# Moving w_phi's load to ScalarE's queue, reordering the first matmuls and moving filler waits in a one-core attention and FFN mix

## The chip, the cores and the metric

One core of one Trainium2 chip. The metric is the device time of one execution in microseconds (us). Single executions of the same kernel stray by 1 us and more here (59 of the kernel before, in one set, took 289.09 to 291.74), so means of many are compared. A run is in the slow state when it took over 1.5% more than the fastest of the same kernel; only one in this study did (293.71 us, granted clock 0.992), and it is left out of the ratios. A "long" execution below is one of the ordinary, fast state that took about 1 us more than most. Where a ratio of two kernels is given, it is the mean time of the one's fast runs over that of the other's of the same rounds; it is not quite the ratio of the medians quoted beside it.

## The reference

Two branches over the same x (2048 tokens of 640 values) are mixed by a gate for each token:

```python
g = sigmoid((x * gate_w).sum(-1, keepdims=True))
# A: qkv = x @ wqkv, 32 heads of 20; q and k go through w_phi (20x20 for each head);
#    phi = concat(softmax(p), softmax(-p)); kv = sum over s of phi_k v; z = sum over s of phi_k
#    o = (phi_q @ kv) / (phi_q . z + 1e-6); a = o @ wo
# B: b = (silu(x @ w_gate) * (x @ w_up)) @ w_down            (F = 1728)
return g * a + (1 - g) * b
```

## The kernel before

The kernel is one long list of items in a fixed order; a recording layer adds a semaphore wait wherever an item needs another engine's result. What the change touches lies almost all in the first 12 us. x tiles 0 to 3 are loaded as they are and transposed on TensorE (item X), VectorE copies them out of PSUM, and V of these four tiles is built up row by row as the rows of wv land (items U tile.row). Dummy matmuls (H, two each) fill TensorE's time while the loads come.

```python
LOADS = "x0 w0 x1 w1 x2 w2 x3 w3 w4 f0 h k0 k1 t4 k2 k3 k4 t5 ..."     # w: wv rows, h: w_phi, k: transposed wk
ORDER = """
H0 H1 a H2 H3 H4 H5 H6 H7 H8 H12 G X0 H9 H10 U0.0 X1 H11 U1.0 U0.1 U1.1 X2 U2.0 U0.2 U1.2 U2.1
X3 U2.2 U0.3 U1.3 U2.3 U0.4 U1.4 U2.4 V3 Y F0.1 M1 i3 M0 F0.0 M2 V4 M3 M4 K0 ...
"""
# G: gate row transposed; Y: w_phi spread into masked blocks wbd; F: an FFN item; M: wk premultiplied with wbd
XQ = ["sp", "act", "act", "act"]; WQ = ["sp", "sp", "sp", "sp", "act"]     # queues of x tiles and wv rows

def load_phi():
    dma("sp", wph[:, :, :], ...)

def act_waits():                       # item a
    for _ in range(NWAIT):             # 88
        act.wait_ge(tr.sem["pe"], 1)   # met as soon as TensorE has done one thing

def v_out(t, pr):                      # evicts V of tile t, frees its PSUM pair
    copy("act", o, i)
    copy("act", svec[:, t:t + 1], bank(2 * pr + 1, 320, 321))

def kv_end():
    for _ in range(NPEW):              # 24
        pe.wait_ge(tr.sem["pe"], 1)
    ...
```

There are four PSUM pairs. V of tiles 0 to 3 holds all of them, so the first FFN item (F0.1) starts only when V of tile 0 has been evicted. The recording layer never asks for an activation table; the toolchain puts one table load ahead of ScalarE's first activation.

The softmax here doesn't subtract the row's maximum and nothing guards it: scores larger than these inputs give would overflow.

## Time and profile before

| | us |
|---|---|
| median of the first 3 runs | 290.37 (290.0 to 291.07) |
| the profiled execution | 289.45, span 288.2 |
| TensorE busy | 284.9 |
| first FFN matmul starts | 12.10 |
| from there to the start of the last matmul | 274.02 |

The lines that carry the reading stand in the prediction below. A line of the chain of waits is: start, length, what ran or was waited for; a line of the timeline is: start, length, engine, source line, operation, output<-inputs, shape, count, and in brackets the engine's idle time before it with what ended it.

### The profile page before, as it was taken

How to read it: one execution, taken by the hardware profiler on the slowest of the kernel's cores; microseconds unless marked ns; L12 is line 12 of the kernel's file. 1: busy time of each engine (PE TensorE's matmuls, PEld its weight loads, DVE VectorE, ACT ScalarE, POOL GpSimd, SP SyncE). 2: the span in 40 equal slices, each digit the busy share in tenths (PEclk: the TensorE clock that was granted, in tenths of full speed). 3: DMA queues.
4: the chain of work that ended last, by engine and by line, in shares of the span. 5: the costliest groups of instructions: out<-in, count | busy, mean ns of one | idle time of the engine just before them, and what ended most of it. 6: DMA issues, size and time to landing. Idle time of an engine off the chain costs nothing.

```text
span 288.2 us, 4961 instructions
## 1 busy us (share of the span) xinstructions
PE 284.9 (99%) x1975; PEld 174.8 (61%) x1975; DVE 163.5 (57%) x243; ACT 151.6 (53%) x252; POOL 159.8 (55%) x125
## 2 busy tenths in 40 slices
PE   8999999999999999999999999999999999999997
PEld 6567777575644445557775556675554446656776
DVE  2146748577469978679991475970317899100000
ACT  0678768666685566583445753225676552234112
POOL 8286899879545789836633438350753558501000
PEclk9999999999999999999999999999999999999999
DMA  6975789000020498302292002061020006210101
GB/s 209 185 113 125 113 212 369 9 0 3 0 50 0 104 306 152 63 2 50 55 165 63 12 1 50 2 144 47 2 50 0 3 1 123 52 45 0 49 23 48
DMA packets 48944, 21.62 MB, mean 75 GB/s; under 512 B 39384, under 2 KB 48792, under 8 KB 48920
## 3 DMA queue, kind: packets, MB, share of 16 engines
q1 hardware_dynamic: 48190, 20.62, 31.5%
q10 hardware_dynamic: 730, 0.68, 0.7%
q8 instruction: 16, 0.26, 0.4%
q14 instruction: 8, 0.07, 0.1%
HBM read 9.29 MB, written 2.62 MB: 41 GB/s over the span
## 4 chain that ended last, share of the span: by engine, by line
PE 98%; ACT 1%; DVE 0%; issue 0%; ACTq 0%
PE ps L296 97%; PE ps L478 1%; PE ps L308 1%; ACT L314 0%; ACT v1r L314 0%; DVE xT L320 0%; DVE osb L730 0%; ACTq L139 0%; ACT svec L314 0%
## 5 line engine op out<-in xcount | busy, mean ns | idle before, releaser
L324 POOL TENSOR_TENSOR hT<-hT,us 128x512 bf16<-128x512 bf16 (+1 forms) x56 | 65.0, 1173 | 67.0 <-DVE hT L328 50.1
L328 DVE SCALAR_TENSOR_TENSOR hT<-hT,ps 128x512 bf16<-128x512 bf16 (+1 forms) x56 | 37.4, 683 | 69.0 <-ACT hT L314 55.3
L296 PE MATMUL ps<-xT,wg 128*128 128x512 bf16 x260 | 64.6, 379 | 0.4 <-ACT svec L314 0.4
L296 PE MATMUL ps<-xT,wu 128*128 128x512 bf16 x260 | 64.6, 379 | 0.0
L296 PE MATMUL ps<-wd,hT 128*128 128x320 bf16 (+2 forms) x462 | 63.9, 295 | 0.0
L324 POOL TENSOR_TENSOR ph<-eq,qc 128x1320 bf16<-128x1320 bf16 x16 | 42.3, 2645 | 25.6 <-DVE qc L638 20.8
L296 PEld LDWEIGHTS ps<-wd,hT 128*128 128x128 bf16 x462 | 44.5, 98 | 17.4
L296 PE MATMUL ps<-wqk,xT 128*128 128x320 bf16 x320 | 47.7, 299 | 0.0
L314 ACT ACTIVATE hT<-ps 128x512 bf16<-128x512 f32 (+2 forms) x60 | 35.8, 597 | 16.0 <-PE ps L296 15.8
L296 PEld LDWEIGHTS ps<-xT,wu 128*128 128x128 bf16 x260 | 25.5, 98 | 30.6
L314 ACT ACTIVATE us<-ps 128x512 bf16<-128x512 f32 (+1 forms) x56 | 33.5, 598 | 19.2 <-PE ps L296 18.2
L296 PEld LDWEIGHTS ps<-xT,wg 128*128 128x128 bf16 x260 | 25.0, 98 | 28.4 <-ACT oT L314 0.8
L314 ACT ACTIVATE osb<-ps,omg 128x640 bf16<-128x640 f32 (+2 forms) x17 | 12.9, 757 | 55.8 <-PE ps L296 55.8
L324 POOL TENSOR_TENSOR ekr<-ekr,krec 128x1280 bf16<-128x1280 bf16 x16 | 37.4, 2357 | 5.7 <-DVE krec L338 5.7
L296 PEld LDWEIGHTS ps<-wqk,xT 128*128 128x128 bf16 x320 | 30.5, 98 | 13.1 <-issue 0.4
L314 ACT ACTIVATE eq<-ps 128x640 bf16<-128x640 f32 x32 | 22.3, 703 | 20.8 <-POOL ph L324 10.6
L335 DVE TENSOR_REDUCE ksum<-ekr 128x64 f32<-128x1280 bf16 x16 | 23.5, 1471 | 11.7 <-ACT ekr L314 11.7
L314 ACT ACTIVATE ekr<-ps 128x640 bf16<-128x640 f32 x32 | 22.3, 703 | 8.7 <-PE ps L296 8.2
L335 DVE TENSOR_REDUCE qz<-eq 128x64 f32<-128x1280 bf16 x16 | 23.7, 1479 | 2.6 <-ACT eq L314 2.6
L296 PE MATMUL ps<-wvg,xT 128*128 128x320 bf16 (+1 forms) x160 | 24.6, 301 | 0.1
L296 PE MATMUL ps<-wog,oT 128*128 128x320 bf16 (+2 forms) x165 | 24.7, 295 | 0.0
L335 DVE TENSOR_REDUCE qw<-ez 128x64 f32<-128x1280 bf16 x16 | 23.6, 1477 | 0.0
(73 smaller groups left out, 189.8 us busy)
## 6 DMA issues: line engine op xcount, KB each, us to landing
out_dram<-osb SPq DMA_DIRECT2D x15, 160.0 KB, 1.9
wd<-in_B_w_down_dram SPq DMA_DIRECT2D x1, 2080.0 KB, 9.5
wg<-in_B_w_gate_dram SPq DMA_DIRECT2D x1, 1040.0 KB, 9.5
wu<-in_B_w_up_dram SPq DMA_DIRECT2D x1, 1040.0 KB, 10.7
wg<-in_B_w_gate_dram SPq DMA_DIRECT2D x1, 800.0 KB, 5.6
wu<-in_B_w_up_dram SPq DMA_DIRECT2D x1, 800.0 KB, 7.2
wog<-in_A_wo_dram SPq DMA_DIRECT2D x2, 375.0 KB, 7.2
wvg<-in_A_wqkv_dram SPq DMA_DIRECT2D x4, 160.0 KB, 4.0
```

What stands on the lines that cost most here:

```text
L296: last = pe.matmul(o, lhsT=l, rhs=r, start=st, stop=sp_, skip_group_check=sk)
L308: last = pe.transpose(o, i, ident[0:k, 0:k])
L314: return run("act", lambda: act.activation(o, i, func, scale=scale), rd, [o])
L324: return run(e, lambda: eo.tensor_tensor(o, a, b, op), [a, b], [o])
L328: return run("dve", lambda: dve.scalar_tensor_tensor(out=o, in0=a, scalar=s, in1=b, op0=op0, op1=op1), rd, [o])
L335: return run("dve", lambda: dve.tensor_reduce(o, i, AX.X, ALU.add), [i], [o])
L478: last = pe.matmul(bank(2 * pr, 0, P), lhsT=c, rhs=c, start=True, stop=True)
```

## The change

Its intent is to have less in TensorE's way in the first 12 us: w_phi leaves SyncE's queue, so that SyncE issues the transposed loads behind it earlier; the transposes of x tile 2 and of the gate row move forward; and the 88 filler waits leave ScalarE's start and come back as six waits in each of the 14 FFN items of the third stage.

```diff
-NWAIT = 88
-NPEW = 24
+NWAIT = 6
+NPEW = 32
@@ ORDER
-H0 H1 a H2 H3 H4 H5 H6 H7 H8 H12 G X0 H9 H10 U0.0 X1 H11 U1.0 U0.1 U1.1 X2 U2.0 U0.2 U1.2 U2.1
+H0 H1 H2 H3 H4 H5 H6 G H7 H8 X0 H9 H10 U0.0 X1 H11 U1.0 U0.1 X2 U1.1 U2.0 U0.2 U1.2 U2.1
@@ (load_rows and dma now return their event; load_wv keeps it in wv_evs)
     def load_phi():
-        dma("sp", wph[:, :, :], ...)
+        tr._wait("act", dict([wv_evs[3]]))
+        dma("act", wph[:, :, :], ...)
@@ (act_waits and item a are gone)
@@ fitem
+        if bt == 2:
+            for _ in range(NWAIT):
+                act.wait_ge(tr.sem["pe"], 1)
         actop(h, g, ACTF.Tanh, 0.5)
```

More of the change, by code (lines that the diff above doesn't have):

```diff
@@ L366, in load_rows @@
     def load_rows(e, dst, c, c0):
-        dma(e, dst, A_wqkv[c * P:(c + 1) * P, c0:c0 + D])
+        return dma(e, dst, A_wqkv[c * P:(c + 1) * P, c0:c0 + D])
     def load_x(t):
@@ L377, in load_ffn @@
         dma("sp", wu[:, :, c0:c1], B_w_up[:, c0:c1].rearrange("(c p) j -> p c j", p=P))
+    wv_evs = []
     def load_wv(c):
-        load_rows(WQ[c], wvg[:, c, 0:D], c, 2 * D)
+        wv_evs.append(load_rows(WQ[c], wvg[:, c, 0:D], c, 2 * D))
     dma("act", gwr[0:5, :], bass.AP(gate_w.tensor, gate_w.offset, [[P, 5], [1, P]]))
     def load_phi():
-        dma("sp", wph[:, :, :], A_w_phi.rearrange("h e f -> (h e) f").rearrange("(c p) f -> p c f", p=P))
+        tr._wait("act", dict([wv_evs[3]]))
+        dma("act", wph[:, :, :], A_w_phi.rearrange("h e f -> (h e) f").rearrange("(c p) f -> p c f", p=P))
     def load_wt(which, m):
@@ L424, in fills @@
             memset("pool", zh[:, NCH:P], 0.0)
-    def act_waits():
-        for _ in range(NWAIT):
-            act.wait_ge(tr.sem["pe"], 1)
     for i in range(3):
@@ L752, in _build @@
         "f": lambda i: load_ffn(FCUT[i], FCUT[i + 1]), "L": load_late_weights, "T": tail_weights, "J": gates,
-        "Y": w_blocks, "a": lambda: act_waits(), "I": kv_begin, "N": kv_end, "Z": z_row,
+        "Y": w_blocks, "I": kv_begin, "N": kv_end, "Z": z_row,
         "Q": qtile, "A": qsum, "B": qden, "C": qscale, "c": qmul,
```

## The prediction

> **What bounds the kernel now.** I read the engines' busy shares and the chain that ended last on the page first, to see who owns the time:
>
> ```profile
> PE 284.9 (99%) x1975; PEld 174.8 (61%) x1975; DVE 163.5 (57%) x243; ACT 151.6 (53%) x252; POOL 159.8 (55%) x125
> ...
> PE 98%; ACT 1%; DVE 0%; issue 0%; ACTq 0%
> ```
>
> TensorE is busy for 284.9 of 288.2 us and is 98% of the chain. Busy does not mean dense, so I also added up what the 1975 matmuls need at 2.4 columns per ns (what warm rows show: x5 of 512 columns in about 1.07 us) and subtracted that from the distances between their starts. The columns need 279.9 us and the distances exceed that by 5.3 us. By fortieths of the span (7.2 us each) the excess is 2.75, 0.72, 0.18, 0.22 and then about 0.1 to 0.3 each, mostly steady issue cost. So **all that can be won lies in the first 12 us**, some 3 us, 1.2% of the span. The chain of waits in order of time shows that stretch:
>
> ```profile
> 6.48 0.07 PE ps L308
> 6.55 0.02 issue
> 6.57 0.23 DVE xT L320
> 6.80 0.05 issue
> 6.85 1.27 PE ps L296 x8
> ...
> 9.95 1.28 ACT L314
> 11.24 0.01 issue
> 11.25 0.71 ACT v1r L314
> 11.95 0.07 ACT svec L314
> 12.02 0.07 issue
> 12.10 66.26 PE ps L296 x616
> ```
>
> Two holes are to be seen. At 6.55 to 6.85 TensorE has transposed x tile 2 and waits for VectorE to copy it out. From 9.8 to 12.1 the chain leaves TensorE: ScalarE loads its activation table (1.28 us), only then evicts the first V tile (0.71 us), and only that frees the PSUM pair for the first FFN matmul, at 12.10. TensorE's other V matmuls run out meanwhile (the last starts at 11.40 and lasts 0.135), so it stands still for 0.57 us. From 12.10 there is not one hole of 0.1 us.
>
> The timeline of ScalarE and of TensorE, cut at these places:
>
> ```profile
> 6.32 0.44 PE L308 MATMUL ps<-ident,xs 128*128 128x128 bf16 x5
> 6.85 1.27 PE L296 MATMUL ps<-wvg,xT 128*128 128x320 bf16 x8
> ...
> 9.95 1.28 ACT L314 ACT_TABLE_LOAD   x1 [9.95 <-PE ps L296]
> 11.25 0.71 ACT L314 ACTIVATE v1r<-ps 128x640 bf16<-128x640 f32 x1
> ```
>
> The table load is shown as released by TensorE, though a table needs no data. The built program tells why: the 88 waits that the kernel puts on ScalarE are packed two to an instruction, together with the real wait for V tile 0 (semaphore value 34), and all of them stand ahead of the table load; the activation behind it keeps only a trivial wait for value 1.
>
> **What the Trainium skill says.** "ScalarE: Activation LUTs", section "What ACT_TABLE_LOAD costs": about 1283 ns for a load, plus some 1380 ns of drain. The trace agrees with the load (1283 ns) and not with a drain: the activation starts 11 ns after it. "Runtime: NRT & Kernel Launch", section "Instruction fetch mechanics": instructions come in 16 KiB blocks by DMA, mostly hidden. The trace has 16 such packets of 16 KB (0.26 MB, the count fits TensorE) and 8 of 8 KB for other engines; they are not free for DMA: at 14.27 one holds a DMA engine 0.96 us and the transposed weight block 2 lands 3.4 us after its issue, not 2.2. "TensorE: Matmul & The Clock Gate", section "What's actually happening": the window that grants full clock is free-running, so the warm-up point varies. Here starts of 128 columns go from 107 to 55 ns apart at about 5.2 us; one trace cannot show the variation. "DMA: Bandwidth & Descriptors", section "Queues, rings and completion order": SyncE and ScalarE each own a queue row over the same DMA engines, served in turn. The page shows two queues (20.6 and 0.68 MB).
>
> **The change, part by part.**
>
> (1) The order of the first items. Before: ... U1.0 U0.1 U1.1 X2 U2.0; after: U1.0 U0.1 X2 U1.1 U2.0. Tile 2's transposes move ahead of U1.1's two matmuls (0.27 us), so VectorE's copy runs under these. X2 would start at 6.04 (its rows landed at 5.56), the copy (start 0.25 after, 0.22 long, 0.05 to signal) ends at 6.57, U1.1 at 6.59: U2.0 starts at 6.59, not 6.85. **Gain 0.26.** Next limits: wv row 2 landed 6.47 (needed 6.87), x tile 3 at 7.56 (needed 7.70, with 0.10 of latency), wv row 3 at 8.05 (needed 8.25). They hold, x tile 3 barely.
>
> (2) The gate row amid the dummies. Before: 20 dummies, gate transpose at 3.07, x tile 0 at 3.18; after: 14 dummies, gate, 4 dummies. The gate row landed at 2.16, so it is ready when 14 dummies are done (about 0.84+14x0.107=2.34). But x tile 0 lands at 3.08, so X0 cannot start before about 3.18, and U0.0 waits for wv row 0 (landed 4.22, start 4.36). **Gain 0.**
>
> (3) The 88 waits go from ScalarE's start. By themselves they were hidden (about 3.2 to 6.5 us, ScalarE idle till 9.8). But in the changed program the real wait for V tile 0 sits on the activation, behind the table load. The table load now waits only for the w_phi issue and a long finished memset.
>
> (4) w_phi on ScalarE's queue. It is issued when wv row 3 has landed (8.05), and took SyncE 0.78 us to issue. So ScalarE is through at about 8.95, the table is in at 10.24, V tile 0 (its last matmul starts at 9.48 now) is evicted by 10.95, FFN could start at about 11.09. TensorE finishes its V matmuls at 11.53-0.26=11.27. So the hole of 0.57 closes with some 0.17 to spare. **Gain 0.57 if w_phi's issue is not held up.** SyncE issues its transposes up to 0.8 us earlier.
>
> (5) 14 FFN items of the third stage get 6 waits each: 3 instructions of two, some 0.08 us apart, 0.23 us an item. ScalarE is busy there 53.0 of 128.2 us (160 to 288) and mostly waits for matmuls: **cost 0**. They put the instruction count back for the tail (360 before, 359 after).
>
> (6) 8 more waits on TensorE's sequencer after K/V: they ran at 0.106 us per two, so 0.42 us more. The sequencer was still about 8 matmuls (1.1 us) ahead after the first 24, so it stays ahead: **cost 0**.
>
> Sum: 0.26+0.57=0.83 off the span, of which I keep 0.75 for (4)'s thin margin. 290.37-0.75=289.6.
>
> **The rivals.** *The queue issue is held up*: SyncE's first transpose took 3.82 us to issue (5.01 to 8.83) behind a full queue. If ScalarE's issue is slow in the same way, the table load slips beyond 10 us and only 0.26 remains: 290.1. For the rival: w_phi is 640 pieces of 40 bytes. Against: before, both queues issued side by side at 0.43 to 0.45 each, and ScalarE's queue is empty by 8.3. *A transfer takes the hole's place*: at 0.83 us earlier the premultiplications come to wait for transposed weights. Slack before: block 2 0.71 (17.04 against 16.33), block 4 0.56. Without SyncE's earlier issue they would miss by up to 0.3; SyncE's earlier issue and the fetch that delays them, itself tied to TensorE's progress, should move along. Worth: 0.1 to 0.3 us back. w_phi itself is no danger: premultiplication starts at 13.4 and the masked blocks took 1.5 us after it landed. *Fetches in new places* delay transfers by 1 to 1.5 us in mid-kernel; most TensorE waits there were met over 1 us early, so little comes of it. *Nothing changes at all*: would need the table load to stay behind TensorE, which the program's order rules out.
>
> **Range and chances.** The mechanism gives 289.5 to 290.1. The three runs before span 290.0 to 291.07, so a median moves by some 0.4 whatever the kernel, in part perhaps by the warm-up's phase. Range 288.9 to 290.5. 2% is 5.8 us: all the idle time of TensorE is less than that, so faster by 2% is nearly excluded; slower would need a new stall of 6 us in a stream that has slack everywhere after 12 us.
>
> **What would show it.** Right: the table load starts at about 9.0, released by the w_phi issue and not by TensorE; the first FFN matmul follows the last V matmul without a hole at about 11.3; U2.0 starts near 6.6; the span is near 287.4. (2) is right if X0 still starts at 3.15 to 3.2. Wrong: table load after 9.5; a hole before the premultiplications at 13 to 18.5; TensorE's gaps near 77 us (from the 8 waits) or in the third FFN stage; or a late warm-up that hides the whole difference.

## The result, and the profile after

The changed kernel took 289.27 us by the median of 6 runs (288.67 to 289.71), the kernel before 290.72 (290.0 to 291.73); ratio 0.9944, 95% interval 0.9918 to 0.997. Its output is correct. By the verdict at 2% it is "same". The profiled execution of the changed kernel has a span of 287.5 us.

The page's busy shares and chain of the changed kernel:

```profile
PE 284.5 (99%) x1973; PEld 174.5 (61%) x1973; DVE 163.5 (57%) x243; ACT 151.8 (53%) x252; POOL 159.8 (56%) x125
...
PE 98%; DMA 1%; SPq 0%; DVE 0%; issue 0%
```

ScalarE is gone from the second line: its 1% was the table load and the first eviction. Its chain of waits in order of time, from x tile 2 on:

```profile
6.32 0.28 PE ps L308 x5
6.60 1.37 PE ps L296 x10
7.97 0.28 PE ps L308 x5
8.25 69.40 PE ps L296 x640
```

Neither VectorE's copy (it stood at 6.57) nor ScalarE's load (it stood at 9.95) is in it: TensorE runs from x tile 2 onward without leaving the chain. The timeline of the changed kernel shows the pieces:

```profile
7.64 0.41 ACTq L350 DMA_DIRECT2D wph<-in_A_w_phi_dram  x1
...
8.14 1.28 ACT L314 ACT_TABLE_LOAD   x1 [8.14 <-DMA wvg<-in_A_wqkv_dram]
...
9.66 0.71 ACT L314 ACTIVATE v1r<-ps 128x640 bf16<-128x640 f32 x1 [0.24 <-PE ps L296]
...
11.39 1.24 PE L296 MATMUL ps<-xT,wg 128*128 128x512 bf16 x5
...
11.73 1.49 POOL L324 TENSOR_TENSOR wbd<-wph,bmask 128x160 bf16<-128x160 bf16 x3 [4.58 <-DMA wph<-in_A_w_phi_dram]
...
13.54 0.79 PE L296 MATMUL ps<-wbd,wT 128*128 128x140 bf16 x12
```

The table load is released by the landing of a wv row now (the wait ahead of w_phi's issue), is done before V of tile 0 is, and the first FFN matmul follows the last V matmul (started at 11.25, 0.134 long) at once, at 11.39. Before it was 12.10. One line gives warning: w_phi landed at 11.65, 1.0 us *later* than before, and the masked blocks made of it were done 0.32 us before the premultiplication at 13.54 read them.

The span fell by 0.7 us; the medians of six runs by 1.45 us. That is nearly twice the holes that the prediction counted (0.83), so either part of the gain lay elsewhere or the six runs were lucky.

### The profile page after: what moved, and what is told of

It is laid out like the page before. It is cut to its first block, busy times and chain, and to the rows that moved or that the text cites. A ratio compares the mean times of both kernels' runs of the same rounds, so it can differ in the third digit from the quotient of the medians.

```text
span 287.5 us, 4960 instructions
## 1 busy us (share of the span) xinstructions
PE 284.5 (99%) x1973; PEld 174.5 (61%) x1973; DVE 163.5 (57%) x243; ACT 151.8 (53%) x252; POOL 159.8 (56%) x125
## 4 chain that ended last, share of the span: by engine, by line
PE 98%; DMA 1%; SPq 0%; DVE 0%; issue 0%
PE ps L296 97%; DMA wvg<-in_A_wqkv_dram 1%; PE ps L308 0%; SPq L350 0%; DVE osb L732 0%; PE ps L477 0%
```

## The experiments

My theory: the gain is the two holes (0.57 us behind the table load, 0.26 us at x tile 2) and nothing else, and the rest of 1.45 us is chance. Rivals: w_phi's way gives part of it; the filler waits cost by their own time; the waits move instruction fetches to better places; the gate row's new place counts. All twelve kernels gave the right result. In each call the kernels share a chip and the runs of the kernel before: 59 runs of 289.78 us median in the first, 58 of 289.78 in the second, 51 of 289.89 in the third, 19 of 290.06 in the last.

What the 14 traces have in common made them easy to read. In 11 of them the distance from the first FFN matmul to the start of the last matmul is 274.01 or 274.02 us, in the other three 274.36, 274.39 and 274.88. So executions differ in how late the first FFN matmul starts, in two kinds of wait behind it, and, once, in the end. (A hole below is the distance between the starts of two matmuls, less what the columns of the first need. "Half clock until" is the end of the last distance at half rate: 107 ns for 128 columns, and 55 ns after.)

| kernel | wv row 0 landed | half clock until | hole at x tile 2 | hole before FFN | first FFN matmul | from there to the last |
|---|---|---|---|---|---|---|
| before | 4.22 | 5.17 | 0.26 | 0.57 | 12.10 | 274.02 |
| before again | 4.16 | 5.32 | 0.26 | 0.57 | 12.10 | 274.02 |
| order only | 5.14 | 8.91 | 0 | 0.57 | 14.07 | 274.01 |
| two waits | 3.88 | 4.92 | 0 | 0.55 | 12.67 | 274.02 |
| no waits | 4.18 | 6.35 | 0.26 | 0 | 12.02 | 274.02 |
| order back | 4.14 | 3.98 | 0.26 | 0 | 11.51 | 274.02 |
| changed | 4.35 | 5.29 | 0 | 0 | 11.39 | 274.02 |
| changed again | 4.40 | 3.88 | 0 | 0 | 11.13 | 274.39 |
| gate back | 3.92 | 3.86 | 0 | 0 | 11.08 | 274.36 |
| w_phi on SyncE | 4.14 | 3.91 | 0 | 0 | 11.45 | 274.88 |
| spread waits undone | 4.93 | 8.97 | 0 | 0 | 13.45 | 274.02 |
| w_phi earlier | 3.94 | 5.21 | 0 | 0 | 11.00 | 274.02 |
| w_phi earlier, dummies | 4.75 | 4.28 | 0 | 0 | 11.41 | 274.02 |
| fewer dummies | 3.85 | 6.02 | 0 | 0 | 12.55 | 274.02 |

### Order back

```diff
-U1.0 U0.1 X2 U1.1 U2.0
+U1.0 U0.1 U1.1 X2 U2.0
```

> The changed kernel with tile 2's transposes back behind U1.1. The theory of the two holes: 0.26 us of the gain is lost, so it is 0.57 us faster than the kernel before where the changed one is 0.83 (by the profile) and U2.0 waits 0.26 us for VectorE's copy again. Rival: the measured gain of 1.45 us (medians) is larger than the two holes because something else, w_phi's way, gives the rest; then this one stays about 1.2 us faster than before.

Measured: 289.49 us median (22 runs), ratio 0.9986 (0.9971 to 1.0), so 0.41 us faster than before, with an interval of 0 to 0.84. The hole at x tile 2 is back, in the timeline of TensorE:

```profile
5.92 0.44 PE L308 MATMUL ps<-ident,xs 128*128 128x128 bf16 x5
6.45 0.45 PE L296 MATMUL ps<-wvg,xT 128*128 128x320 bf16 x2
7.09 1.00 PE L296 MATMUL ps<-wvg,xT 128*128 128x320 bf16 x6 [0.20 <-DMA wvg<-in_A_wqkv_dram]
```

The third line shows where such a gain can go. Here wv row 2 landed at 7.05 and TensorE waited for it right behind the hole, so closing the hole would have won nothing in this execution. The mean lies on the theory's side (0.57) of the rival's 1.2, which the interval excludes.

### Two waits

The changed kernel with two always met waits on ScalarE, recorded ahead of its first activation.

```diff
+    def act_waits():
+        for _ in range(2):
+            act.wait_ge(tr.sem["pe"], 1)
-H0 H1 H2
+H0 H1 a H2
```

> The changed kernel with two waits on ScalarE that are always met, ahead of the first eviction. The theory: they are packed with the real wait for V tile 0, all stand ahead of the table load, so the load starts only when TensorE has finished V tile 0 (about 9.5 us), and the hole of 0.57 us before the first FFN matmul is back: 0.26 us faster than the kernel before. Rival (the 88 waits cost by their own time, not by where they put the table load): two waits are 0.08 us, and nothing changes against the changed kernel, 1.45 us faster than before.

Measured: 289.9 us, ratio 1.0008 (0.9993 to 1.0023): the gain is gone. The chain of waits:

```profile
1.73 4.79 DMA wvg<-in_A_wqkv_dram
...
10.52 1.28 ACT L314
11.80 0.01 issue
11.82 0.71 ACT v1r L314
12.52 0.07 ACT svec L314
12.59 0.08 issue
12.67 66.26 PE ps L296 x616
```

The table load is behind TensorE again, with the same 1.28 and 0.71 us after it and the same hole of 0.55 us. Two waits of together less than 0.1 us do what 88 did, so it is not their own time. In the built program of this kernel (the list of each engine's instructions that the toolchain makes, with the semaphore values they wait for) the real wait for V of tile 0 is packed into the instructions ahead of the table load and the activation keeps "at least 1"; in the changed kernel it is on the activation. The rival is excluded. The mean came out 0.23 us slower than before, not 0.26 faster; the interval's faster end is 0.20, so the 0.26 of the order of items is not seen in this mean. This execution lost 0.82 us to wv row 1, which landed at 6.52.

### No waits

```diff
-NWAIT = 88
+NWAIT = 0
```

This is the kernel before, with nothing else changed.

> The kernel before with the 88 waits taken away and nothing else: the table load moves to about 3.3 us. The theory: the hole of 0.57 us closes, 0.57 us faster than before, the wait of 0.26 us at x tile 2 stays. Rival (w_phi's way or the spread waits give the gain): less than 0.3 us.

Measured: 289.55 us (14 runs), ratio 0.999 (0.9969 to 1.0012), which is 0.29 us faster and leaves both readings open. The trace decides. The timeline of ScalarE:

```profile
5.01 1.28 ACT L314 ACT_TABLE_LOAD   x1 [5.01 <-POOL v1r L342]
10.30 0.71 ACT L314 ACTIVATE v1r<-ps 128x640 bf16<-128x640 f32 x1 [4.00 <-PE ps L296]
```

Without the waits the table is in at 6.3 and ScalarE then waits 4 us for V. The hole before the FFN is 0. Taking the waits away is by itself enough; w_phi's way is not needed for it. (The load came at 5.0 rather than 3.3: a memset of GpSimd's stands ahead of it.)

### Order only

The kernel before with X2 ahead of U1.1.

> The kernel before with tile 2's transposes ahead of U1.1 and nothing else. The theory: 0.26 us faster than before, and the hole before the first FFN matmul stays at 0.57 us. Rival (the hole behind the table load is set by something that does not move with TensorE): the hole grows to 0.83 us and nothing is gained.

Measured: 289.84 us (14 runs), ratio 1.0001 (0.9987 to 1.0016): no gain by the mean; the interval, 0.38 us faster to 0.46 slower, holds the 0.26 too. In the trace the hole at x tile 2 is gone and the hole of 0.57 us before the FFN stays, as expected. But it is a long execution, 291.41 us, and shows what can make one long. The timeline of TensorE:

```profile
3.70 0.63 PE L478 MATMUL ps<-const-bfloat16-1.0 128*128 128x128 bf16 x4
5.27 0.70 PE L296 MATMUL ps<-wvg,xT 128*128 128x320 bf16 x2 [0.94 <-DMA wvg<-in_A_wqkv_dram]
...
6.51 1.28 PE L296 MATMUL ps<-wvg,xT 128*128 128x320 bf16 x4
...
14.07 0.81 PE L296 MATMUL ps<-xT,wg 128*128 128x512 bf16 x3 [0.40 <-ACT svec L314]
```

wv row 0 landed at 5.14 and TensorE stood still for some 1.1 us; four V matmuls at 6.51 then take 0.27 us each, twice the warm 0.135, and half rate lasts until 8.91. The wait and the slow clock together put the first FFN matmul 2 us later than in the two traces of the kernel before.

### The changed kernel and the kernel before, again

> The changed kernel once more, unaltered. In the trace of every kernel so far the stretch from the first FFN matmul to the last matmul is 274.01 or 274.02 us, and two executions differ only in when that matmul starts: 12.10 (before), 11.39 (changed), 11.51, 12.67, 12.02, 14.07 (experiments), by how late wv rows land and when TensorE's clock comes up. The theory: the gain is 0.83 us less what late rows hide, 0.6 to 0.8 us by the mean of many runs, and the 1.45 us of the first six runs was chance. Rival: it is 1.45 us again, and some part of the gain is not in the two holes.

> The kernel before, unaltered, against itself: how far a ratio of fast runs strays by chance, and a second trace of it. Theory: ratio within 0.0015 of 1; the hole of 0.57 us at the table load and that of 0.26 us at x tile 2 stand in the trace again, wherever the clock comes up, and from the first FFN matmul to the last it is 274.02 us.

Measured: the changed kernel 289.37 us (13 runs), ratio 0.9976 (0.9958 to 0.9995), **0.70 us faster** by the mean, 0.41 by the medians. The kernel before against itself: 290.21 (22 runs), ratio 1.0008 (0.9989 to 1.0027), and its trace repeats the first one to 0.02 us in both holes. So a ratio can stray by some 0.25 us by chance even over 22 runs, and the 1.45 us of the first six runs did not come again.

The changed kernel's second trace holds what I had not expected, though. Its timeline:

```profile
12.03 0.82 DVE L324 TENSOR_TENSOR wbd<-wph,bmask 128x160 bf16<-128x160 bf16 x2 [3.50 <-DMA wph<-in_A_w_phi_dram]
12.08 1.49 POOL L324 TENSOR_TENSOR wbd<-wph,bmask 128x160 bf16<-128x160 bf16 x3 [4.93 <-DMA wph<-in_A_w_phi_dram]
12.21 1.24 PE L296 MATMUL ps<-xT,wu 128*128 128x512 bf16 x5
...
13.67 0.79 PE L296 MATMUL ps<-wbd,wT 128*128 128x140 bf16 x12 [0.21 <-issue]
```

The clock came up early, TensorE reached the FFN at 11.13, and then stood for w_phi: landed 12.00, masked blocks done 13.57, premultiplication at 13.67 where it could have begun at 13.29. That is the 0.37 us by which this trace exceeds 274.02. The bracket says "issue", as the profile found no releaser; that the blocks' semaphore came 0.09 us before the matmul, and all else that it waited for over 0.8 us before, names it.

### w_phi on SyncE

```diff
-        tr._wait("act", dict([wv_evs[3]]))
-        dma("act", wph[:, :, :], ...)
+        dma("sp", wph[:, :, :], ...)
```

> The changed kernel with w_phi back on SyncE's queue. The table load then waits for nothing but ScalarE's DMA issues and comes at 3.3 to 5 us. The theory: the gain comes from where the table load stands, not from the way of w_phi, so no hole before the first FFN matmul and the time of the changed kernel (within 0.2 us); w_phi lands about 10.5 us, 1 us earlier than in the changed kernel's trace (11.65), and the margin before the first premultiplication grows from 0.32 us to above 1. Rival: w_phi's way is the cause of part of the gain, and 0.3 us or more is lost.

Measured: 289.1 us (14 runs), ratio 0.9971 (0.9951 to 0.9991), 0.84 us faster than before. The gain does not need w_phi's move. As expected w_phi landed earlier (10.94) and its margin was 1.1 us. But its trace has another wait, in the chain:

```profile
14.55 4.65 DMA wT<-in_A_wqkv_dram
19.20 0.05 issue
19.25 59.32 PE ps L296 x562
```

Block 4 of the transposed wk was issued at 14.55 and landed at 19.20, and TensorE lost 0.85 us. In the changed kernel, where w_phi's issue is out of SyncE's way, it was issued at 12.65 and landed at 17.23, 1.1 us before its use. It took about as long there (4.58 us, and 4.89 in the second trace), so what sets the two kernels apart is the issue, 1.5 to 1.9 us later here. An instruction fetch of 16 KB ran beside the block in each of these traces (here at 16.96, for 1.2 us). In the 14 traces the block took 3.1 to 3.6 us from the end of its issue in nine of the ten where a fetch began between 0.2 us before that end and 1.5 us after it, 1.7 us in the tenth, and 2.2 to 2.8 us in the other four. That speaks for the fetch as a second cause of the late landing, but no run tests it. So, by one trace of this kernel, w_phi's move guards one transfer at the cost of another, and neither shows in the mean.

### Spread waits undone

```diff
-NWAIT = 6
-NPEW = 32
+NWAIT = 0
+NPEW = 24
```

> The changed kernel without the 84 waits of the third FFN stage and with 24 instead of 32 waits on TensorE after K/V. The theory: both lay beside TensorE's work, so the time is the changed kernel's within 0.2 us and the stretch from the first FFN matmul to the last stays 274.02 us. Rival (the waits move instruction fetches to better places, above all at the end): 0.3 us or more slower, seen behind the last matmul.

Measured: 289.36 us (22 runs), ratio 0.9979 (0.9962 to 0.9997), 0.61 us faster than before; 274.02 us to the last matmul, and 2.10 us from there to the end, as in the changed kernel (2.10). The spread waits and the eight on TensorE cost nothing and give nothing that shows. This trace is a long execution as well: wv row 0 at 4.93, half clock until 8.97.

### Gate back

```diff
-H0 H1 H2 H3 H4 H5 H6 G H7 H8 X0
+H0 H1 H2 H3 H4 H5 H6 H7 H8 G X0
```

> The changed kernel with the gate row's transpose back behind all the dummies. The theory: x tile 0 lands at about 3.08 and wv row 0 at 4.15 to 4.4 whatever stands before them, so nothing changes: X0 within 0.07 us of 3.15, the time of the changed kernel within 0.2 us (some 0.7 us faster than before). Rival: the gate row amid the dummies is worth something (fewer gaps, an earlier clock), and 0.3 us or more is lost.

Measured: 289.24 us (22 runs), ratio 0.9981 (0.9962 to 0.9999), 0.55 us faster than before, not to be told from the changed kernel; X0 at 3.13. The gate row's place is worth nothing. The trace has the wait for w_phi too (landed 11.91, 274.36).

### w_phi earlier, and with more dummies

```diff
-        tr._wait("act", dict([wv_evs[3]]))
+        tr._wait("act", dict([wv_evs[2]]))
```

> The changed kernel with w_phi issued on ScalarE's queue when wv row 2 has landed (6.5) and not row 3 (7.6 to 8.0). In the second trace of the changed kernel TensorE was early (first FFN matmul 11.13), w_phi landed at 12.00, the masked blocks were done at 13.57 and the first premultiplication waited 0.37 us for them. The theory: w_phi lands 1 us earlier, below 11, that wait is gone in every execution, and the late block 4 of the transposed weights (the kernel with w_phi on SyncE's queue waited 0.85 us for it) stays away since SyncE's queue is as in the changed kernel: up to 0.3 us faster than the changed kernel by the mean, from the first FFN matmul to the last 274.02 us. Rival: w_phi's small pieces now go beside the wv rows and make these later by as much.

Measured: 289.13 us (14 runs, 3 of them above 290.7), ratio 0.9982 (0.9959 to 1.0006). In its trace TensorE was the earliest of all, at the FFN at 11.00, and still did not wait:

```profile
11.43 1.49 POOL L324 TENSOR_TENSOR wbd<-wph,bmask 128x160 bf16<-128x160 bf16 x3 [4.27 <-DMA wph<-in_A_w_phi_dram]
...
13.15 0.79 PE L296 MATMUL ps<-wbd,wT 128*128 128x140 bf16 x12
```

That is 274.02 again and the shortest span of the study, 287.1 us. But w_phi landed at 11.36, not below 11. It was issued 1.2 us earlier than in the changed kernel's first trace (6.47 against 7.64), yet its first packet ran at 10.01, against 10.19 there. It moved only as the FFN weights in SyncE's queue ran out (w_up landed at 10.16 and 9.95); that these held it back was not tested, and SyncE's first transposed block was under way too by then, from 8.4 and 8.2 on. In the seven traces with the issue behind wv row 3 the first packet came 2.1 to 2.4 us after the issue's end, here 3.2. By the mean nothing is shown.

The next kernel has the same edit and two more dummy items:

```diff
-X0 H9 H10 U0.0
+X0 H9 H10 H13 H14 U0.0
```

> The same with four more dummy matmuls between x tile 0 and the first V matmul (0.43 us at half clock). In the two slowest traces wv row 0 landed at 4.93 and 5.14, TensorE stood about 1 us, and its clock came up only at 8.9 us, not at 3.9 to 6.3: 2 us in all. Theory: the dummies fill the wait, the clock comes up at the earlier time more often, and the share of executions above 290.7 us (15% of those before) falls, for less than 0.15 us by the median. Rival: the late clock has another cause, or 0.43 us do not fill enough, and the dummies only delay the first V matmul where wv row 0 is in time (0.1 us slower).

Measured: 289.2 us (22 runs, the slowest 290.32), ratio 0.9971 (0.9957 to 0.9985), 0.84 us faster than before. None of 22 lies above 290.7, against 8 of the 51 runs of before and 3 of the 14 without the dummies beside it. In its trace wv row 0 was late (4.75), and half clock ended at 4.28 all the same; with the dummies TensorE stood only 0.33 us for it.

### Fewer dummies

The opposite, to test the cause of the "slow tail" (the executions above 290.7 us): the changed kernel without H9 and H10.

> The changed kernel without the four dummy matmuls that stand between x tile 0 and the first V matmul: TensorE then stands still 0.43 us longer there, 0.7 to 0.9 us where wv row 0 lands as usual. The theory of the slow tail (a wait of about 1 us there keeps the clock down to 8.9 us, one of 0.5 us does not): executions above 290.7 us become much more common, from 0 of 13 (changed kernel) and 23 of 168 (kernel before, three sets) to 40% or more, and the mean rises by 0.5 us or more, though the work has grown less. Rival: the clock comes up at a time of its own, whatever stands there, and the share stays at 10 to 20%.

(The count of 23 in this text was a slip: 9 + 9 + 8 is 26 of 168.)

Measured: 290.9 us (14 runs, one of them in the slow state), ratio of the fast runs 1.0012 (0.9992 to 1.0031). 8 of 14 lie above 290.7, or 7 of the 13 fast ones, against 3 of 19 of before: the share is 54 to 57%. Less work on TensorE took the whole gain of the change away: by the mean the kernel is 0.35 us slower than before (from 0.23 faster to 0.90 slower). The trace of the profiled execution lost its time otherwise; the chain:

```profile
1.80 5.47 DMA xs<-in_A_x_dram
7.27 0.05 issue
7.32 0.45 PE ps L308 x5
```

x tile 2 landed at 7.27, and at the end one piece of the last store landed at 290.51, 1.9 us after the others. Nor does it have the stop that the theory speaks of: wv row 0 was early (3.85), TensorE stood 0.34 us for it, and half clock ended at 6.02. So the share of long executions supports the cause, while the one trace of this kernel doesn't show it.

**A version that beats both?** The kernel with w_phi earlier and more dummies beats the kernel before clearly. Against the changed kernel it was not run on the same chip; ratios of 0.9971 and 0.9976 to the same kernel before don't part them. What it has is the missing tail, and even that is not shown against the changed kernel itself, which had 0 of 13 executions above 290.7 us; the five near copies without extra dummies (order back, w_phi on SyncE, spread waits undone, gate back, w_phi earlier) had 15 of 94.

## Why the prediction was right

Predicted were 289.6 us (288.9 to 290.5) and a gain of about 0.75; measured were 289.27 and, by the larger set of runs, 289.37, with a gain of 0.70 (interval 0.14 to 1.22). That the time itself came so near is in part luck. The 289.6 was reckoned from three runs of the kernel before (290.37), and the five later sets of it have medians of 289.78 to 290.21; from 289.78 the same sum gives 289.0. The range was wide enough to hold no change at all. What bears the mechanism out is the holes in the traces.

- **The table load behind TensorE, by how waits are packed: right and shown.** It moved to 8.14 (8.95 was foreseen), two waits put it back, and taking the 88 away is enough. The hole is 0.55 to 0.57 in the four traces with the load behind TensorE and 0 in the ten others.
- **The order of the first items: right in the traces, not shown in the means.** The hole of 0.26 us is there in the four traces with U1.1 first and in no other. Order only gained 0.0 ± 0.4 us. Rows that land late can take the gain back, as in "order back"; how often stays open.
- **The gate row: 0, right.** x tile 0 started at 3.12, gated by its landing at 3.07.
- **The issue on ScalarE's queue: right, with room.** It took 0.41 us, not 0.78, and the table was in early enough in every trace.
- **Waits spread and added: 0, right.**
- **The step that failed: "w_phi itself is no danger".** I took the landing before (10.64) and expected no later one, with the two queues served in turn. It landed at 11.65 to 12.39 in the seven traces with the changed kernel's issue of it, and in the two of them where TensorE reached the FFN earliest (11.13 and 11.08) the premultiplication waited 0.34 to 0.37 us. In the means this loss is not seen. The rival "a transfer takes the hole's place" had about the right size (0.1 to 0.3 foreseen) but named the wrong transfer: with SyncE freed, the transposed blocks kept 1.1 and 0.5 us of room in the two traces.
- **A sum that is wrong without harm.** The columns do not need 279.9 us but 275.5, and the distances exceed that by 9.8 and not 5.3: 20 times in the kernel before, two half-array matmuls of 512 columns start 3 to 10 ns apart and run side by side, and the prediction counted both. The excess by fortieths is read rightly, but the first two come to 3.5 us, not "some 3".
- **The noise: right in size, its cause only guessed at.** In the traces it is late landings at the start (wv row 0 together with the clock, up to 2 us; wv row 1, 0.8; x tile 2, 1.0) and once the last store, 1.9.

## What to carry to other kernels

Look at what stands ahead of a one-time load in the built program: a wait that is always met can be packed with a real one and pull the load behind data that it doesn't need. When all of the gain lies in the first few microseconds, separate the deterministic body from the head in each trace; one trace then shows where a hole is or is not, as twenty timings here did not, though what closing it is worth by the mean still takes many runs. Try filling TensorE's wait for its first operand with dummies: in the two traces where it stood about 1 us there, half clock lasted to 8.9 and 9.0 us, in the other twelve to 6.35 at most, and the stop and the clock together cost some 2 us.

## What the Trainium skill lacked or had wrong

- "ScalarE: Activation LUTs", section "What ACT_TABLE_LOAD costs": the load of 1283 ns is confirmed (1283 ns). Its drain of about 1380 ns is not seen at this first load of the kernel: in the kernel before the activation started 11 ns after the load's end.
- No page that I read has it that always met waits ahead of a first activation can move the wait for its data ahead of the table load: 0.57 us here, from two waits as from 88.
- "TensorE: Matmul & The Clock Gate", section "What's actually happening", gives ±500 ns for the warm-up point. Half rate ended between 3.86 and 8.97 us in 14 traces of nearly the same first matmuls; the two latest were those in which TensorE stood about 1 us for wv row 0, and without them it is 3.86 to 6.35.
- "DMA: Bandwidth & Descriptors", section "Queues, rings and completion order", has each DMA engine go round between the queue rows that have work. w_phi's 640 packets of 40 bytes on ScalarE's row, issued at 6.47 or 7.64, ran only from 10.01 and 10.19 on, when SyncE's FFN weights were nearly or all through: 2.1 to 3.2 us after the issue's end. The traces don't show when its descriptors stood ready, so this need not contradict the page; what held it is open.
- "Runtime: NRT & Kernel Launch", section "Instruction fetch mechanics": the fetches of 16 KB are there (16 of them), and 8 of 8 KB on another queue, a size that it doesn't give for refills. It calls crossing a block "mostly hidden"; for other transfers on the same DMA engine that need not hold, as a fetch takes 0.88 to 1.73 us. That the fetch had a part in the 0.85 us that TensorE stood for block 4 was not tested.
